# A delta-rule attention with two MoE layers on one core: low words on VectorE, conversions behind the preparation's copies, a MoE lag of two chunks, a fence

## The chip, the cores and the metric

The kernel runs on one core of a Trainium2 chip as a single launch. The metric is device time in microseconds (us). Its engines are PE (TensorE, matmuls; PEld is its weight loads), DVE (VectorE), ACT (ScalarE), POOL (GpSimd) and SP (SyncE, which here only issues transfers). Each engine works through its own list of instructions in order; the lists are bound to each other by semaphores.

## The reference, cut to what matters

```python
# attention, 4 batches x 8 heads, 768 steps, 48 x 48 state per head
y[:, :, t] = q_t @ state
state += beta_t * outer(k_n_t, v_t - state^T k_n_t)
# first layer, 3072 tokens
h = (x @ w1) * (x @ w2) @ w3 @ w_out          # 384 -> 1024 -> 1024 -> 384
# second layer
h = x @ w_in                                   # 384 -> 1024
solu = h * softmax(h)
out = (layernorm(solu) * g_ln) @ w_out2        # 1024 -> 384
```

The weights are 64-bit floats. A piece of them is loaded as two 32-bit words per number, and turned into 32-bit floats on the chip ("conversion").

## The kernel before, in words

Attention is done in chunks of 64 steps (48 chunks, `c`), two at a time: chunks of even and odd `c` belong to two pairs of batches. Three stages share the engines until about 730 us.

**The start (to about 155 us).** `prep(i)` brings k and q of two chunks into the layouts that the chain wants: PE transposes (`pk`, `pq`, lines 258 and 265), ACT copies (260 to 270), products of k with k and q (`pg`, 276), and ACT copies of those (278 to 281, `GD`, `G`). `pk`, `pq` and `pg` share two PSUM buffers. Four such steps fill `GD` for eight chunks, a "set". `invert(n)` then solves 128 triangular systems on DVE in 62 small steps that depend on each other (315, 321), between a transpose of `GD` (`Lz`, 305) and transposes of the result (`Dt` 326, `D1n` 327). Beside all this `conv` steps through the generator `wg`, which converts the weights piece by piece: first `w_out` (8 pieces of 384 columns), then `w3` (16 pieces of 512, transposed on PE as `w3p`, copied as `area`, and multiplied into `w3 @ w_out`, `wps`, line 517, whose result `Ws` is split into two parts by `split`, 217 and 218), then `w1` and `w2` (12 pieces of 512, split in the same way). A piece passes `start` (ACT: the high word, 134; ACT: the low word, 137), `middle` (DVE: a shift, 141) and `finish` (DVE: an add, 178, seen in the profile as CUSTOM_DVE). The pieces share five buffers, so a later load waits until an earlier piece is used up.

**The main loop (chunks two at a time).** `merge` makes the matrices `TW` of a chunk (342 to 381), `chain_u`, `chain_s` and `chain_y` are the recurrence (407, 430, 447, with copies into `X` at 412, 413, 436, 437 and the result `xb` at 457, 458). `load_v`, the copies `kst<-ktok` and the loads of k and q go through SP's queue. The preparation and the inversion of the next set are mixed in. `moe_block(j)` is the first layer for 256 tokens (four chunks): 144 matmuls `pab` (542) and 72 matmuls `px` (562). `fill_moe` hands out its steps. Block `j` may begin in the program when `c_done` has reached `4 * (j + 1) + LAG` and 8 chunks are done.

**The rest** is the end of the first layer and the second layer, where PE has no gaps worth naming.

What sets the order: a tile framework schedules all instructions when the program is built, by their place in the program and a model of their times. An instruction that stands late in the program is put early if its engine is free in that model and its inputs are there. So an edit in one place moves instructions on every engine. `tc.issue_after(ins)` makes all instructions of the block that run on `ins`'s engine stand behind `ins`. `tc.no_sync_barrier()` keeps what stands behind it in the program behind what stands ahead of it, engine by engine, without a semaphore.

Of the kernel before, what the change touches and what calls it, by code (L numbers as in the profile page):

```python
# [8 lines left out]
F32 = mybir.dt.float32  # L9
F32R = mybir.dt.float32r  # L10
U32 = mybir.dt.uint32
I64 = mybir.dt.int64
AF = mybir.ActivationFunctionType
ALU = mybir.AluOpType
# [6 lines left out]
def kernel(  # L21
# [15 lines left out]
    nc = tc.nc  # L37
# [4 lines left out]
    C = 64  # L42
    HC = 32
# [12 lines left out]
    SB = 4  # L56
    CA = 8
    CD = 8
    LAG = 4
    P0, C0 = 4, 24  # L60
    LO = 2
    WO, WB = 2, 15
# [1 line left out]
    KA = 64 + D  # L64
# [32 lines left out]
    QA = at.tile([128, RQ, NP, 2, C], F32, tag="QA", name="QA")  # L97
# [12 lines left out]
    def kt_of(i):  # L110
        return ktoks.get(i, ktok[i % 2])
# [17 lines left out]

    def start(raw, o, n, out):  # L130
        w = raw[:, 2 * o:2 * (o + n)].rearrange("p (n two) -> p n two", two=2)
        low = raw[:, 2 * o:2 * o + n]
        t = out(n)
        nc.scalar.activation(
            out=t, in_=w[:, :, 1].bitcast(F32), func=AF.Prelu, scale=2.0 ** -112, alpha=2.0 ** 32
        )
        nc.scalar.activation(out=low, in_=w[:, :, 0], func=AF.Copy, scale=2.0 ** -29)
        return low, t.bitcast(U32)

    def middle(low, u):  # L140
        nc.vector.tensor_scalar(
# [5 lines left out]
    def convert(items, out, queue=None, behind=0):  # L147

        items = list(items)
        words, holder, pend = {}, {}, []
        nxt = [0]

        def fetch(done, end=len(items)):
            while nxt[0] < end:
                i = nxt[0]  # L160
                slot, parts, w = items[i][:3]
                if slot in holder and holder[slot] >= done:
                    return
                st = slot()[:, 0:2 * w]
                for r, src in parts:
                    d = st.bitcast(I64)[r]
                    if len(src.shape) == 3:
                        d = d.rearrange("p (a d) -> p a d", a=src.shape[1])
                    (queue(i, src) if queue else nc.sync).dma_start(out=d, in_=src)
                words[i] = st.bitcast(U32)  # L170
                holder[slot] = i
                nxt[0] += 1

        def finish():
            i, o, low, u = pend.pop(0)
            n = u.shape[1]
            value = items[i][5](o, n) if len(items[i]) > 5 else low.bitcast(F32)
            nc.vector.tensor_tensor(out=value.bitcast(U32), in0=u, in1=low, op=ALU.add)
            yield
            items[i][4](o, value)  # L180
            yield
            if o + n == items[i][2]:
                fetch(i + 1)

        if behind:
            fetch(0, 1)
            yield
        fetch(0)
        yield
        todo = [(i, o, n) for i, it in enumerate(items) for o, n in it[3]]  # L190
        ahead = []
        for z in range(len(todo) + behind):
            if z < len(todo):
                i, o, n = todo[z]
                if i not in words:
                    while ahead:
                        i2, o2, st = ahead.pop(0)
                        got = yield from middle(*st)
                        pend.append((i2, o2) + got)
                    while pend and i not in words:  # L200
                        yield from finish()
                    fetch(i - 1)
                ahead.append((i, o, start(words[i], o, n, out)))
            if len(ahead) > behind or z >= len(todo) and ahead:
                i, o, st = ahead.pop(0)
                got = yield from middle(*st)
                pend.append((i, o) + got)
                if len(pend) > 1:
                    yield from finish()
        while pend:  # L210
            yield from finish()
# [43 lines left out]
    def prep_t(i):  # L255
        pk = ps_prep.tile([128, NP, 128], F32, tag="prep", name="pk")
        for p in range(NP):
            nc.tensor.transpose(pk[:, p, :], kt_of(i)[:, p, :], ident)
        r = pk.rearrange("r p (c t) -> r c p t", c=2)
        nc.scalar.copy(out=KQ[0:KA, :, :, 0:C], in_=r[0:KA])  # L260
        nc.vector.tensor_copy(out=KB[0:D, :, :, C:128], in_=r[0:D])
        nc.scalar.copy(out=KB[64:KA, :, :, 0:C], in_=r[64:KA])  # L262
        pq = ps_prep.tile([128, NP, 128], F32, tag="prep", name="pq")
        for p in range(NP):
            nc.tensor.transpose(pq[:, p, :], qt_of(i)[:, p, :], ident)
        r = pq.rearrange("r p (c t) -> r c p t", c=2)
        nc.scalar.copy(out=KQ[0:KA, :, :, C:128], in_=r[0:KA])
        sl = chunk_of(i) % RQ
        nc.scalar.copy(out=QA[0:64, sl:sl + 3:2, :, 1, :], in_=r[0:64])
        nc.scalar.copy(out=QA[64:KA, sl:sl + 3:2, :, 0, :], in_=r[64:KA])  # L270

    def prep_g(c):
        cc, sl, u0 = c % 4 // 2, c % RQ, c % SETC * NP
        pg = ps_prep.tile([128, NP, 128], F32, tag="prep", name="pg")
        for p in range(NP):
            nc.tensor.matmul(pg[:, p, :], KB[0:KA, cc, p, :], KQ[0:KA, cc, p, :], start=True, stop=True)  # L276
        gd = GD[:, u0:u0 + NP, :]
        nc.scalar.copy(out=gd[:, :, :], in_=pg[:, :, 0:HC])
        nc.scalar.copy(out=G21[:, sl], in_=pg[:, :, 0:HC])
        nc.scalar.copy(out=gd[32:64], in_=pg[32:64, :, HC:C])  # L280
        nc.scalar.copy(out=gd[96:128], in_=pg[96:128, :, HC:C])  # L281
        for h in range(2):
            r = slice(64 * h, 64 * h + 64)
            nc.vector.tensor_tensor(  # L284
                out=QA[r, sl, :, h, :], in0=pg[r, :, C:128],
                in1=mask[r].unsqueeze(1).to_broadcast([64, NP, C]), op=ALU.mult,
            )
# [362 lines left out]
    for h in range(2):  # L650
        nc.gpsimd.affine_select(
            out=mask[64 * h:64 * h + 64], in_=mask[64 * h:64 * h + 64], pattern=[[1, C]],
# [5 lines left out]
    c_done = [0]  # L658
    acc = [0.0]

    def conv(x, ins=None):
        acc[0] += x
        if acc[0] < 1:
            return
        with (tc.issue_after(ins.ins) if ins is not None and c_done[0] >= CA else nullcontext()):
            while acc[0] >= 1:
                next(wg, None)
                acc[0] -= 1
# [24 lines left out]
    for i in range(SETC // 2):  # L693
        for k_, _ in enumerate(prep(i)):
            if k_ == 0 and i > 0 and i + 1 < SETC // 2:
                norm(i + 1)
            conv(P0)

    for ins in invert(0):
        conv(0.5, ins)  # L700
    invert_end(0)
# [5 lines left out]
    def moe_all():  # L707
        for j in range(NTB):
            while c_done[0] < min(CPT * (j + 1) + LAG, NCH) or c_done[0] < CD:
                yield "wait"  # L710
# [12 lines left out]

    PLAN, PLAN0 = ((0,), (1,), (2, 3), ()), ((), (0, 1), (2, 3), ())
    inv_gen = iter(())
    for c in range(0, NCH, 2):
        n, s = c // SETC, c % SETC
        last = s == SETC - 2
# [214 lines left out]
```

## Time and profile before

| what | us |
|---|---|
| median of 3 runs | 958.99 (954.17 to 960.03) |
| profiled execution, its own time | 959.24 |
| its span, first to last instruction | 957.5 |
| PE busy in the span | 871.8 |
| DVE busy | 597.8 |
| ACT busy | 552.4 |

The mean granted clock of TensorE is 0.959 of full speed. The span is shorter than the time of the execution by 1.74 us. A busy PE is one that has a matmul under way, at whatever clock.

### The profile page before, as it was taken

Reading aid. Unit: us, or ns where it says so; the run is one execution under the profiler, and the core shown is the slowest. Engines: PE = TensorE matmul, PEld = TensorE weight load, DVE = VectorE, ACT = ScalarE, POOL = GpSimd, SP = SyncE. Lnnn points to the kernel's source line nnn. Section 1 sums busy time; section 2 is a strip of 40 time slices with the busy share of each in tenths; the row PEclk is TensorE's granted clock in tenths of the full one; section 3 lists DMA queues with packets and bytes.
Section 4 is the critical chain, followed back from the end, with each engine's and each line's share of the span. In section 5 each row is a group of like instructions: output and inputs, shape, how many; then the busy total and the mean of one; then the engine's idle time right before and its main releaser. Section 6 shows DMA issues by size and latency. Waiting matters only on the chain.

```text
span 957.5 us, 23008 instructions
## 1 busy us (share of the span) xinstructions
PE 871.8 (91%) x9104; PEld 775.8 (81%) x9104; DVE 597.8 (62%) x1500; ACT 552.4 (58%) x1481; POOL 43.7 (5%) x99
## 2 busy tenths in 40 slices
PE   2788669998899899989999999999999999999998
PEld 2554457897789788978888888879999989999997
DVE  5677743695379657944597559765653655555553
ACT  6984688727673786376635873585643444343433
POOL 5100000000000000000000000000000100000000
PEclk9999757999799999997999999999999999999999
DMA  9799313320242133222220321133422212122110
GB/s 242 254 200 151 58 28 58 67 50 11 55 88 45 35 63 66 48 49 54 54 55 22 65 43 36 50 91 96 147 69 84 67 58 66 60 73 67 58 34 34
DMA packets 141691, 70.65 MB, mean 74 GB/s; under 512 B 109712, under 2 KB 133520, under 8 KB 139792
## 3 DMA queue, kind: packets, MB, share of 16 engines
q1 hardware_dynamic: 139808, 57.64, 26.6%
q0 software_dynamic: 1776, 11.54, 3.5%
q8 instruction: 72, 1.18, 0.5%
q14 instruction: 35, 0.29, 0.1%
HBM read 47.91 MB, written 14.25 MB: 65 GB/s over the span
## 4 chain that ended last, share of the span: by engine, by line
PE 33%; issue 22%; ACT 18%; DVE 16%; DMA 7%; POOL 2%; SPq 1%; POOLq 0%; ACTq 0%; DVEq 0%
PE pab L542 10%; PE px L562 6%; ACT TW L342 4%; DVE Tt L321 3%; DVE tmp L315 3%; PE uy L407 3%; PE pm L376 2%; DMA ktok<-in_k_dram 2%; PE wps L517 2%; DVE asg L550 1%; PE pst L430 1%; DMA raw_w2s<-in_moe_w_dram 1%; PE pg L276 1%; PE uy L447 1%; PE ph L833 1%
## 5 line engine op out<-in xcount | busy, mean ns | idle before, releaser
L542 PE MATMUL pab<-xb,w1s 128*128 128x256 f32 x864 | 132.0, 291 | 2.2 <-DVE asg L550 2.1
L542 PE MATMUL pab<-xb,w2s 128*128 128x256 f32 x864 | 129.2, 288 | 0.0
L562 PE MATMUL px<-gh,Ws 128*128 128x256 f32 x864 | 126.7, 293 | 2.1 <-DVE xs L218 1.6
L542 PEld LDWEIGHTS pab<-xb,w1s 128*128 128x128 f32 x864 | 114.3, 193 | 5.3 <-DVE asg L550 3.2
L562 PEld LDWEIGHTS px<-gh,Ws 128*128 128x128 f32 x864 | 110.4, 193 | 7.1 <-DVE xs L218 3.3
L542 PEld LDWEIGHTS pab<-xb,w2s 128*128 128x128 f32 x864 | 113.4, 192 | 1.3
L886 PE MATMUL po<-w4s,ln 128*128 128x384 f32 x576 | 105.7, 339 | 0.3 <-ACT ot L892 0.3
L833 PE MATMUL ph<-wis,x 128*128 128x512 f32 x432 | 105.7, 398 | 0.0
L886 PEld LDWEIGHTS po<-w4s,ln 128*128 128x128 f32 x576 | 101.4, 188 | 2.8 <-ACT ot L892 0.5
L833 PEld LDWEIGHTS ph<-wis,x 128*128 128x128 f32 x432 | 79.5, 189 | 16.9 <-issue 0.2
L849 ACT ACTIVATE e<-ph,nm 128x1024 f32<-128x1024 f32 x24 | 26.8, 1117 | 87.5 <-DVE nm L848 86.0
L342 ACT COPY TW<-Dt 32x128 f32<-32x128 f32 x192 | 56.7, 295 | 15.7 <-DVE Dt L326 12.9
L321 DVE TENSOR_TENSOR Tt<-Tt,tmp 128x31 f32<-128x31 f32 (+15 forms) x186 | 63.1, 340 | 3.5
L315 DVE TENSOR_TENSOR tmp<-Lz,Tt 128x31 f32<-128x31 f32 (+15 forms) x186 | 63.0, 338 | 3.5 <-DVE xp L355 0.2
L549 ACT COPY asg<-pab 128x256 f32<-128x256 f32 x96 | 35.6, 371 | 48.5 <-PE pab L542 42.9
L551 ACT CAST gh<-asg 128x256 fp32r<-128x256 f32 x96 | 38.9, 405 | 37.7 <-DVE asg L550 37.2
L284 DVE TENSOR_TENSOR QA<-pg,mask 64x256 f32<-64x256 f32 x96 | 40.5, 422 | 31.9 <-ACT GD L281 29.3
L276 PE MATMUL pg<-KQ,KB 112*128 112x128 f32 x384 | 53.8, 293 | 3.1 <-ACT KB L262 2.4
L276 PEld LDWEIGHTS pg<-KQ,KB 112*128 112x128 f32 x384 | 49.3, 205 | 7.4 <-ACT KB L262 5.6
L848 DVE TENSOR_REDUCE nm<-ph 128x1 f32<-128x1024 f32 x24 | 29.4, 1225 | 40.4 <-PE ph L833 40.4
L517 PE MATMUL wps<-area 128*128 128x384 f32 x128 | 47.1, 518 | 4.7 <-ACT area L512 2.6
L550 DVE TENSOR_TENSOR asg<-pab,asg 128x256 f32<-128x256 f32 x96 | 40.5, 422 | 17.4 <-ACT asg L549 15.3
(147 smaller groups left out, 1379.6 us busy)
## 6 DMA issues: line engine op xcount, KB each, us to landing
x2d<-xs SPq DMA_DIRECT2D x72, 128.0 KB
x<-x2d SPq DMA_DIRECT2D x24, 384.0 KB
X<-in_v_dram SPq DMA_DIRECT2D x96, 48.0 KB
out_dram<-ot SPq DMA_DIRECT2D x24, 192.0 KB
ktok<-in_k_dram SPq DMA_DIRECT2D x44, 96.0 KB
qtok<-in_q_dram SPq DMA_DIRECT2D x44, 96.0 KB
kst<-ktok SPq DMA_DIRECT2D x88, 48.0 KB
raw_w2s<-in_moe_w_dram POOLq DMA_DIRECT2D x4, 1024.0 KB, 10.3
```

Of the source, the lines that this page charges most:

```text
L276: nc.tensor.matmul(pg[:, p, :], KB[0:KA, cc, p, :], KQ[0:KA, cc, p, :], start=True, stop=True)
L284: nc.vector.tensor_tensor(out=QA[r, sl, :, h, :], in0=pg[r, :, C:128], in1=mask[r].unsqueeze(1).to_broadcast([64, NP, C]), op=ALU.mult,)
L315: yield nc.vector.tensor_tensor(out=t, in0=Lz[:, j, j + 1:HC].unsqueeze(2).to_broadcast([128, m, j + 1]), in1=Tt[:, j, 0:j + 1].unsqueeze( ...
L321: yield nc.vector.tensor_tensor(out=Tt[:, j + 1:HC, 0:j + 1], in0=Tt[:, j + 1:HC, 0:j + 1], in1=t, op=ALU.add)
L342: nc.scalar.copy(out=TW[r, tw, :, g // 2, o:o + HC], in_=Dt[r, us, :])
L517: nc.tensor.matmul(acc[m], w3t[:, j, :], wos[kk // (NF // 2)][:, kk % (NF // 2), :], start=(kk == 0), stop=(kk == NF - 1),)
L542: nc.tensor.matmul(pab[:, e, :], ws[m][:, a, fs], xb[:, b, m, :], start=(n == 0), stop=(n == 3 * NM - 1), skip_group_check=True,)
L550: nc.vector.tensor_tensor(out=g, in0=pab[:, 1, :], in1=asb, op=ALU.mult)
L551: nc.scalar.copy(out=gh[:, 0, f, :], in_=g)
L562: nc.tensor.matmul(px, Ws[:, a, f, js], gh[:, b, f, :], start=(n == 0), stop=(n == 3 * NF - 1),)
L833: nc.tensor.matmul(ph[:, gs], x2[:, m, a, :], wis[:, b, m, gs], start=(n == 0), stop=(n == 3 * NM - 1),)
L886: nc.tensor.matmul(po, ln[:, a, f, :], w4s[:, b, f, :], start=(n == 0), stop=(n == 3 * NF - 1),)
```

## The change: what it does

Four edits.

- In `start` the low word (`w[:, :, 0]`, scaled and rounded to an integer) is made by DVE instead of ACT, into the tile `t`, which before took the high word. The high word is written by ACT over the raw words. `t` and the raw area change their roles in `middle` and `finish`.
- While `held[0]` is set, what `conv` issues on ACT stands behind the last copy that `prep_t` or `prep_g` has issued. `held[0]` is cleared before the first inversion.
- `LAG` goes from 4 to 2.
- A fence stands at the head of the main loop.

```diff
-    LAG = 4
+    LAG = 2
...
     def start(raw, o, n, out):
         w = raw[:, 2 * o:2 * (o + n)].rearrange("p (n two) -> p n two", two=2)
-        low = raw[:, 2 * o:2 * o + n]
-        t = out(n)
+        high = raw[:, 2 * o:2 * o + n]
+        t = out(n).bitcast(U32)
+        nc.vector.tensor_scalar(
+            out=t, in0=w[:, :, 0], scalar1=2.0 ** -29, scalar2=None, op0=ALU.mult
+        )
         nc.scalar.activation(
-            out=t, in_=w[:, :, 1].bitcast(F32), func=AF.Prelu, scale=2.0 ** -112, alpha=2.0 ** 32
+            out=high.bitcast(F32), in_=w[:, :, 1].bitcast(F32), func=AF.Prelu,
+            scale=2.0 ** -112, alpha=2.0 ** 32,
         )
-        nc.scalar.activation(out=low, in_=w[:, :, 0], func=AF.Copy, scale=2.0 ** -29)
-        return low, t.bitcast(U32)
+        return t, high
...
-            value = items[i][5](o, n) if len(items[i]) > 5 else low.bitcast(F32)
+            value = items[i][5](o, n) if len(items[i]) > 5 else u.bitcast(F32)
...
-        nc.scalar.copy(out=QA[64:KA, sl:sl + 3:2, :, 0, :], in_=r[64:KA])
+        held[0] = nc.scalar.copy(out=QA[64:KA, sl:sl + 3:2, :, 0, :], in_=r[64:KA])
...
-        nc.scalar.copy(out=gd[96:128], in_=pg[96:128, :, HC:C])
+        held[0] = nc.scalar.copy(out=gd[96:128], in_=pg[96:128, :, HC:C])
...
-        with (tc.issue_after(ins.ins) if ins is not None and c_done[0] >= CA else nullcontext()):
+        with (tc.issue_after(ins.ins) if ins is not None and c_done[0] >= CA else tc.issue_after(held[0].ins) if held[0] is not None else nullcontext()):
...
+    held[0] = None
     for ins in invert(0):
...
     inv_gen = iter(())
+    tc.no_sync_barrier()
     for c in range(0, NCH, 2):
```

In the changed kernel a line number is higher by 3 from `start` on (278 is 281 there), and by 5 to 7 after `conv`. The new DVE instruction has line 134, the high word on ACT line 137.

ACT, behind the first preparation's copies of q (`QA<-pq`): `stage_a` and `raw_w2s` are weights that are being converted, `GD` and `G_93` the copies of the first `pg`. Before, in the order of the list:

```order
L134 ACTIVATE t<-stage_a 128x384 x2
L137 ACTIVATE stage_a<-stage_a 128x384 x2
L134 ACTIVATE t<-raw_w2s_163 128x384 x2
L137 ACTIVATE raw_w2s_163<-raw_w2s_163 128x384 x2
L134 ACTIVATE t<-raw_w2s_165 128x384 x2
L137 ACTIVATE raw_w2s_165<-raw_w2s_165 128x384 x2
L278 COPY GD<-pg 128x128
L279 COPY G_93<-pg 128x128
L280 COPY GD<-pg 32x128
L281 COPY GD<-pg 32x128
```

And now:

```order
L243 ACTIVATE sq<-early 128x384
L245 ACTIVATE ss<-ss 128x8
L137 ACTIVATE stage_a<-stage_a 128x384
L281 COPY GD<-pg 128x128
L282 COPY G_93<-pg 128x128
L283 COPY GD<-pg 32x128
L284 COPY GD<-pg 32x128
L137 ACTIVATE stage_a<-stage_a 128x384
L137 ACTIVATE raw_w2s_163<-raw_w2s_163 128x384
```

The copies of `pg` stood behind all eight pieces of `w_out`; now they stand behind three.

DVE, from the first `X` copy of the main loop on (`chain_u` of chunk 0). Before, the copy of chunk 1 is three rows further on:

```order
L413 COPY X<-uy 64x4x48
L178 ISA stage_a<-t,stage_a 128x1024
L218 TENSOR_TENSOR w2s_951<-stage_a,w2s_951 128x512
L413 COPY X<-uy 64x4x48
L218 TENSOR_TENSOR w2s_951<-stage_a,w2s_951 128x512
```

Now (the first twelve rows; the copy of chunk 1 is the 29th):

```order
L416 COPY X<-uy 64x4x48
L144 TENSOR_SCALAR raw_w2s_697<-raw_w2s_697 128x512
L221 TENSOR_TENSOR w1s_922<-raw_w2s_647,w1s_922 128x512
L181 ISA raw_w2s_647<-raw_w2s_647,t 128x1024
L134 TENSOR_SCALAR t<-stage_a 128x512
L144 TENSOR_SCALAR raw_w2s_697<-raw_w2s_697 128x512
L181 ISA raw_w2s_697<-raw_w2s_697,t 128x1024
L221 TENSOR_TENSOR w1s_922<-raw_w2s_647,w1s_922 128x512
L134 TENSOR_SCALAR t<-stage_a 128x512
L221 TENSOR_TENSOR w1s_937<-raw_w2s_697,w1s_937 128x512
L144 TENSOR_SCALAR raw_w2s_697<-raw_w2s_697 128x512
L181 ISA raw_w2s_697<-raw_w2s_697,t 128x1024
```

The last pieces of `w1`, which were converted during the first inversion, stand behind the fence, and with those of `w2` between the two `X` copies.

PE, between the steps of `merge` for chunks 28 and 29 (`pm`). Before:

```order
L562 MATMUL px<-gh,Ws 128x256 x5
L360 MATMUL pm<-xp,D1n 32x32 x8
L542 MATMUL pab<-xb,w2s_966 128x256 x2
L542 MATMUL pab<-xb,w2s_989 128x256 x3
L542 MATMUL pab<-xb,w1s_814 128x256 x3
L360 MATMUL pm<-xp,D1n 32x32 x8
L542 MATMUL pab<-xb,w1s_921 128x256 x3
L376 MATMUL pm<-TW,kst 48x64 x8
L542 MATMUL pab<-xb,w1s_936 128x256
L376 MATMUL pm<-TW,kst 48x64 x8
```

And now (a part of it; from the last `pst` of chunk 27 to the first `uy` of chunk 28 there are 101 `pab` in all):

```order
L363 MATMUL pm<-xp,D1n 32x32 x8
L545 MATMUL pab<-xb,w1s_814 128x256 x3
L545 MATMUL pab<-xb,w1s_922 128x256 x3
L545 MATMUL pab<-xb,w1s_937 128x256 x2
L363 MATMUL pm<-xp,D1n 32x32 x8
L545 MATMUL pab<-xb,w1s_937 128x256
L545 MATMUL pab<-xb,w2s_952 128x256 x3
L545 MATMUL pab<-xb,w2s_967 128x256 x3
L545 MATMUL pab<-xb,w2s_990 128x256 x3
```

From the first `uy` of chunk 26 to that of chunk 28 there were 12 `pab` and 14 `px`, now 106 `pab`. It is alike from chunk 34 to 36 and from 42 to 44 (20 and 13 `pab` before, 119 and 112 now). From chunk 10 to 12 there were 9 of the two together, now 23. Between the last `pg` of a set and the first `pm` that needs its inversion the number of MoE matmuls stays within 9 of what it was (249 and 249, 253 and 244, 248 and 246 for three of the sets).

## Rows read from the trace of the kernel before

**Rows 1.** The page: its first line, and busy time by engine.

```profile
span 957.5 us, 23008 instructions
PE 871.8 (91%) x9104; PEld 775.8 (81%) x9104; DVE 597.8 (62%) x1500; ACT 552.4 (58%) x1481; POOL 43.7 (5%) x99
```

**Rows 2.** Windows of the start: length; busy PE, PEld, DVE, ACT, POOL; clock, DMA, GB/s.

```profile
10.75:62.06 51.31, 35.23 (x161) 26.21 (x162) 34.48 (x71) 46.58 (x107) 10.56 (x19) 1.00 0.91 250
62.06:108.14 46.08, 35.01 (x120) 20.68 (x118) 39.59 (x103) 22.52 (x44) 2.46 (x5) 0.92 0.89 150
110.04:154.96 44.92, 33.08 (x528) 28.24 (x529) 16.39 (x31) 38.63 (x110) 0.96 (x1) 0.54 0.17 32
```

**Rows 3.** Timeline: start, duration, engine, line [idle before, releaser].

```profile
24.47 0.27 ACT L278 COPY GD<-pg 128x128 f32<-128x128 f32 x1
26.61 1.09 PE L258 MATMUL pk<-ident,ktok 128*128 128x128 f32 x4 [10.06 <-ACT GD L281]
39.49 1.96 SPq L299 DMA_DIRECT2D bl<-bd  x4
```

**Rows 4.** Chain of waits: start, duration, what.

```profile
66.84 13.86 DMA raw_w2s<-in_moe_w_dram
390.36 1.81 DMA xb<-xb
```

**Rows 5.** Timeline of ACT and DVE around the first inversion and the first chunks.

```profile
60.88 0.26 ACT L281 COPY GD<-pg 32x128 f32<-32x128 f32 x1
62.06 2.00 DVE L305 STREAM_TRANSPOSE Lz<-GD 128x1024 f32<-128x1024 f32 x1
81.50 0.43 DVE L141 TENSOR_SCALAR t<-t 128x512 uint32<-128x512 uint32 x1 [2.95 <-ACT t L134]
108.14 1.90 DVE L326 STREAM_TRANSPOSE Dt<-Tt 128x1024 f32<-128x1024 f32 x1
120.49 0.36 DVE L413 COPY X<-uy 64x192 f32<-64x192 f32 x1
154.08 0.53 ACT L412 COPY X<-uy 64x192 f32<-64x192 f32 x2
```

**Rows 6.** Groups by shape, to 140 us: busy, ns of one | idle.

```profile
L137 ACT ACTIVATE raw_w2s<-raw_w2s 128x512 uint32<-128x512 uint32 x14 | 9.0, 673 | 0.0
L141 DVE TENSOR_SCALAR t<-t 128x512 uint32<-128x512 uint32 x28 | 12.7, 456 | 18.6 <-ACT t L134 17.9
L178 DVE CUSTOM_DVE_ANT_0 raw_w2s<-t,raw_w2s 128x1024 uint16<-128x1024 uint16 x14 | 9.4, 686 | 1.2 <-ACT raw_w2s L137 1.0
L218 DVE TENSOR_TENSOR w1s<-raw_w2s,w1s 128x512 fp32r<-128x512 f32 x6 | 4.1, 687 | 0.0
L217 ACT CAST w1s<-raw_w2s 128x512 fp32r<-128x512 f32 x6 | 3.6, 619 | 3.6 <-PE wps L517 1.8 <-DVE raw_w2s L178 1.7
```

**Rows 7.** Timeline of DVE: the instruction after the first transpose.

```profile
64.28 1.22 DVE L308 SCALAR_TENSOR_TENSOR Lz<-Lz,bl 128x1024 f32<-128x1024 f32 x1
```

**Rows 8.** Windows of chunks 10, 18, 26 and 34.

```profile
233.72:255.16 21.44, 17.96 (x314) 15.14 (x310) 9.53 (x27) 15.51 (x50) 0.00 (x0) 0.81 0.25 47
333.72:347.75 14.03, 12.95 (x241) 11.26 (x241) 7.87 (x21) 12.34 (x40) 0.00 (x0) 1.00 0.28 55
425.78:443.07 17.29, 16.07 (x240) 13.95 (x239) 8.38 (x22) 12.31 (x39) 0.00 (x0) 0.77 0.30 62
533.43:547.90 14.47, 13.94 (x254) 12.57 (x253) 9.31 (x25) 12.32 (x40) 0.00 (x0) 1.00 0.35 72
```

**Rows 9.** Windows of 4 us around the second fall of the clock in the loop.

```profile
432.00:436.00 4.00, 2.78 (x66) 2.43 (x62) 3.06 (x9) 3.77 (x15) 0.00 (x0) 0.87 0.17 29
436.00:440.00 4.00, 4.00 (x45) 3.42 (x44) 2.46 (x8) 2.33 (x10) 0.00 (x0) 0.50 0.24 46
```

**Rows 10.** Waits of PE from 228 to 700 us: total, times, longest.

```profile
PE pm L360 <- DVE xp L355: 9.4, 18, 1.5
```

**Rows 11.** Window of the last chunks, where `w_in` is converted.

```profile
624.00:672.00 48.00, 46.09 (x743) 41.58 (x737) 28.35 (x81) 34.65 (x107) 0.00 (x0) 1.00 0.34 96
```

More of the change, by code (lines that the diff above doesn't have):

```diff
@@ L659 @@
     acc = [0.0]
+    held = [None]
     def conv(x, ins=None):
```

## The prediction

> **What bounds the kernel now.** I read the page first [rows 1]: PE is busy for 871.8 of 957.5 us, so all that a reordering can win is 85.7 us of idle PE, and time in which PE is busy at the lower clock. Next come windows of each stage. About half of the idle time lies ahead of 155 us, the rest almost all in the loop between 190 and 700 us; behind that PE has no gaps. So two questions decide: when the start lets the loop go (its mark is the `X` copy of chunks 4 and 5, at 154.08 [rows 5]), and at which clock and with how few gaps the loop runs.
>
> The start is bound by three lists one after the other [rows 2]. To `Lz` it is ACT: 46.58 of 51.31 us busy. The next `pk` waits 10.06 us for the `GD` copies, which stand in ACT's list behind all of `w_out`'s conversions [rows 3]; the last `GD` copy ends at 61.1 and `Lz` starts at 62.06 [rows 5]. Through the inversion it is DVE: 39.59 of 46.08 us busy in 103 instructions. The largest part of the rest is a stall of 2.95 us in front of the first `w1` piece [rows 5]: its transfer takes 13.86 us and lands at 80.7 [rows 4]. From 110 to 155 it is ACT again, 38.63 of 44.92, while DVE has only 16.39.
>
> [...]
>
> **The change part by part.** All sums stand against the profiled execution, 959.24 us, which is the median of the runs (958.99) to within 0.25.
>
> *Conversions behind the preparation's copies.* The first `GD` copy now stands behind three pieces of `w_out` instead of eight. Five pieces at two passes of some 0.6 us are 6 us: it comes at about 18.6 instead of 24.47, and `pk` follows. But the gain isn't carried whole to `Lz`. The copy `Tt<-bl` (line 310) now stands ahead of the copies of the last two preparations, and `bl` is issued by SP only from 39.49 to 41.45 [rows 3]; with a small transfer's 1.81 us [rows 4] it is there at about 43.5. Behind it are some 30 ACT instructions, about 12.5 us of list. So the last `GD` ends near 56, `Lz` starts near 57: 5 us earlier. The other end: a wait for `bl` that costs all of it, 0.
>
> *The low word on DVE.* ACT loses 36 passes in the start (8 of 384 columns, 28 of 512; 0.673 us each [rows 6]), DVE gains 36 that read every second word. No row shows that operation on DVE. The low bound is a shift of the same 512 columns, contiguous: 0.43 to 0.46 us [rows 5, 6]. The high bound is half of the strided transpose `Lz`, 2.00 us for 1024 [rows 5]: 1.00; the contiguous operation of 1024 right behind it takes 1.22 [rows 7]. I take 0.61, a little less than the two-input subtraction of 512 columns, 0.687 [rows 6], which also reads more than one word per result. Ends kept: 0.43 and 1.00.
>
> [...]
>
> *The inversion.* DVE's list from `Lz` to `Dt` gains nine low words (5.5 us) and one shift (0.46), and loses four subtractions for `w1` (2.75), one for `Ws`, one add (0.69) and the normalisations of two preparations (3.0), which now stand elsewhere: -0.65 us net, so 39 us of busy time and some 2 us of small gaps. In it the first `w1` piece is reached at 74.5 to 76. Its transfer landed at 80.7; it starts when a buffer comes free and SP has issued it, up to 4 us earlier now, so 76 to 80.8; I take 78.4, a stall of about 4 us. `Dt` then starts at 102 to 104 against 108.14: 4.5 us gained of the 5.
>
> *Behind the fence.* The pieces of `w1` and `w2` that now stand between the `X` copies of chunks 0 and 1 on DVE (27 instructions, some 16 us) put the second copy about 25 us behind the start of the loop instead of 10.5 (120.49 less 110.04 [rows 5, 2]). That is covered: ACT's list up to `X(c4,c5)` is longer. It had 38.63 us in 44.92 [rows 2]; six low words leave it (-3.4 to -4), one high word (0.9 with its wait), four casts at 0.62 [rows 6] (2.1 to 2.5), the cast of `Ws` (0.4) and two normalisations (1.4) come to it, so it has 40 to 41.5 us of work, and `X(c4,c5)` comes 42.5 to 43 us behind the loop's start instead of 44. Gain 1.5 us. If DVE's pieces were each 0.4 longer, the cover would be used up. Altogether the start is 6 us shorter; bounds: 9 shorter (no stall for `w1`, cheap low words) and 2 longer (`bl` late, low words near 0.8).
>
> SP's queue: the transfers `kst<-ktok` for chunks 4 and 5 are moved past those of `xb` and the loads of `v`. POOL's: a memset of `Tt` stands in front of one load of weights. Both at nothing: the second set's preparation waits for its normalisation, and the weights for a buffer. If that cover went, each would be one small transfer, 1.8 us [rows 4].
>
> *The low words of `w_in` and `w_out2`* (20 of 256 or 384 columns) lie under a PE that is busy for 46.09 of 48.00 us, with DVE at 28.35 [rows 11]: nothing. Without that cover 20 times 0.3 to 0.6, 6 to 12 us.
>
> *The lag.* The MoE work is the same; only its place moves. Between chunk 26 and 28 there are now 106 `pab` where there were 12 and 14 `px`. At a fall that came when PE had 2.78 us of work in 4 [rows 9] this is the work that was missing. Window 26 lost 17.29 less 14.3, 3 us, and about as much behind it until 450 us: 6.5 us gained. The fall at chunk 10 (21.44 against 14.03) stays, as there are only 23 matmuls of the MoE there now instead of 9, and no block can start before eight chunks are done. PE's waits for `xp` in `merge` are 9.4 us in 18 places [rows 10]; with more MoE work between a few of them I take 1 us. Bounds for the loop: 0 and -14 (both falls gone).
>
> **Sum**: 959.24 - 6 - 6.5 - 1 = 945.7, so 946.
>
> **The rivals.**
>
> 1. *Slower: the low word is dear on DVE.* At 1.00 us instead of 0.61 [rows 5] the 36 of the start cost 14 us more, all of them on the list that bounds the inversion or ahead of the third `X` copy, where the cover is 16 of 42 us. The start is then 8 us longer instead of 6 shorter, and if the loop gives nothing the time is 967. It decides from where -6 + 36 (x - 0.61) = 0, x = 0.78 us. For it: `Lz` against its neighbour [rows 7]. Against: DVE is idle for 16.8 of the 51.31 us ahead of `Lz` [rows 2] and for more behind `Dt`, which take a part. Chance 0.10, 957 to 968.
> 2. *The start gains, the loop doesn't.* The work that is put in at chunk 26 is missing at 28 (36 `pab` there instead of 140), so the fall moves there or to 36 and 44, where now nothing falls [rows 8]. 959.24 - 6 = 953; 950 to 957, chance 0.25.
> 3. *`w1` lands when it did.* The 13.86 us transfer is the same, and if it lands at 80.7 again the inversion keeps all but 2 to 3 us of its old end; the loop gains. 959.24 - 2.5 - 6.5 - 1 = 949.3; 947 to 952, chance 0.15.
> 4. *Both falls go.* 946 less 7 = 939; 935 to 941, chance 0.10. Against: the 23 matmuls.
>
> **How the numbers follow.** My forecast, 946 with 938 to 950 as its own range, has 0.40. The range to hold 8 times in 10 takes in the second and the third rival and the fourth, and the cheap half of the first: 935 to 960. A measurement of this kernel tells 1%, 9.6 us, from no change: faster means under 949.4. That holds nearly all of the forecast, the fourth rival and part of the third: 0.53. Slower, above 968.6, is the dear end of the first rival with a little for what I don't see: 0.07. The rest, 0.40, is no difference that can be told.
>
> **What would show it.** In the changed profile: the first `GD` copy near 18.6 and `Lz` near 57 (the first step); the mean of the new DVE line for 512 columns, 0.61, where 0.78 or more speaks for the first rival; a stall of about 4 us at the first `w1` piece and `Dt` at 102 to 104 (61 or later for `Lz`, 107 or later for `Dt`, and the third rival or worse holds); the second `X` copy far behind the first with nothing waiting, and `X(c4,c5)` near 147 to 148; a granted clock of 1.00 from chunk 26 to 30, with a window of about 14.3 us, and the fall at chunk 10 still there. I am wrong if the clock falls in another pair, if PE is idle between the `X` copies of chunks 0 and 1 because of DVE and the third comes after 154, or if the last set's chunks end later because a MoE block has been used up earlier.

## The result and the profile after

The changed kernel takes 941.30 us (median of 4 executions, 939.07 to 942.89), the one before 956.58 (953.57 to 960.03): a ratio of 0.9845, 95% interval 0.9804 to 0.9886. In the last set of experiments the same kernel took 944.39 against 956.38, with a ratio of 0.9845 (0.9793 to 0.9897). A ratio here is an estimate from the single executions, without those more than 1.5% above the fastest of their kernel, and not the quotient of the two medians, which for this second set would be 0.9875. The forecast was 946.

The page of the profile after, its first line and the busy time by engine, against [rows 1]:

```profile
span 940.7 us, 23008 instructions
PE 864.9 (92%) x9104; PEld 770.7 (82%) x9104; DVE 613.0 (65%) x1556; ACT 525.9 (56%) x1425; POOL 43.6 (5%) x99
```

The span is 16.8 us shorter. PE's busy time fell by 6.9 us and its idle time, span less busy, from 85.7 to 75.8. ACT lost 26.5 us of work and DVE gained 15.2.

The windows that answer to [rows 2, 8] (length; busy PE, PEld, DVE, ACT, POOL; clock, DMA share, GB/s): to `Lz`; from `Lz` to `Dt`; from the first `TW` copy to the `X` copy of chunk 5; on to the second `Lz`; 30 us with the fall of the clock in the loop; and 40 us in which chunk 26 lies.

```profile
12.71:60.85 48.14, 34.82 (x156) 26.77 (x157) 34.04 (x81) 33.69 (x81) 10.26 (x19) 1.00 0.94 253
60.85:101.38 40.53, 33.94 (x123) 20.31 (x122) 37.12 (x100) 14.66 (x26) 2.46 (x5) 1.00 0.98 174
103.34:145.90 42.56, 29.52 (x549) 25.24 (x550) 28.42 (x57) 39.77 (x114) 0.96 (x1) 0.60 0.07 14
145.90:177.03 31.13, 29.55 (x402) 26.64 (x402) 16.88 (x41) 27.95 (x88) 0.00 (x0) 1.00 0.47 90
205.00:235.00 30.00, 28.61 (x400) 25.04 (x399) 16.02 (x41) 17.98 (x58) 0.95 (x1) 0.77 0.08 18
406.00:446.00 40.00, 38.57 (x598) 34.49 (x596) 19.40 (x50) 30.48 (x95) 0.00 (x0) 1.00 0.26 55
```

Up to `Lz` ACT is busy for 33.69 of 48.14 us, where it had 46.58 of 51.31. The inversion is 40.53 us long instead of 46.08. The third row is the stage in which ACT was the bound; it is still busy for 39.77 of 42.56. In the loop this execution has one fall (0.77 between 205 and 235 us, at chunk 8; the two falls before lay at chunks 10 and 26), and chunk 26 runs at 1.00. Its pair is not shorter for that: from its first `uy` (418.39) to that of chunk 28 (441.74) it is 23.35 us, with 106 `pab` in it, where before it was 17.29.

The marks on ACT and on DVE, in the timeline (start, duration, engine, line; in brackets the idle time before and what ended it), against [rows 3, 5]:

```profile
20.26 0.27 ACT L281 COPY GD<-pg 128x128 f32<-128x128 f32 x1
43.22 0.25 ACT L310 COPY Tt<-bl 128x32 f32<-128x32 f32 x1 [0.37 <-issue]
46.40 0.48 ACT L220 CAST Ws<-wps 128x384 fp32r<-128x384 f32 x1 [2.93 <-PE wps L520]
...
142.67 0.30 ACT L415 COPY X<-uy 64x192 f32<-64x192 f32 x1
145.59 0.31 ACT L415 COPY X<-uy 64x192 f32<-64x192 f32 x1
```

```profile
60.85 1.96 DVE L308 STREAM_TRANSPOSE Lz<-GD 128x1024 f32<-128x1024 f32 x1
79.53 0.43 DVE L134 TENSOR_SCALAR t<-raw_w2s 128x512 uint32<-128x512 uint32 x1 [2.24 <-DMA raw_w2s<-in_moe_w_dram]
...
101.38 1.93 DVE L329 STREAM_TRANSPOSE Dt<-Tt 128x1024 f32<-128x1024 f32 x1
112.54 0.36 DVE L416 COPY X<-uy 64x192 f32<-64x192 f32 x1 [4.80 <-ACT X L415]
128.64 0.36 DVE L416 COPY X<-uy 64x192 f32<-64x192 f32 x1
```

The first `GD` copy comes at 20.26 instead of 24.47, `Lz` only 1.2 us earlier than before, `Dt` 6.8 earlier, the `X` copy of chunk 4 11.4 earlier (chunk 5, which before was copied in one row with it, 8.8). The second `X` copy on DVE stands 16.1 us behind the first with conversions between them; ACT is idle for only 2.8 us of the stage, so its list should hide that, but no run moves these pieces alone. The second `Lz` is at 177.03 against 185.38: 8.3 us of the 16.8 are won by then.

The new instruction, by shape up to 140 us (busy, mean ns of one | idle before), with the shift of the same 512 columns and the high word on ACT, against [rows 6]:

```profile
L134 DVE TENSOR_SCALAR t<-raw_w2s 128x512 uint32<-128x512 uint32 x14 | 6.4, 468 | 2.2 <-DMA raw_w2s<-in_moe_w_dram 2.2
L144 DVE TENSOR_SCALAR raw_w2s<-raw_w2s 128x512 uint32<-128x512 uint32 x14 | 5.8, 420 | 3.5 <-ACT raw_w2s L137 3.4
L137 ACT ACTIVATE raw_w2s<-raw_w2s 128x512 f32<-128x512 f32 x14 | 9.2, 671 | 4.5 <-DVE t L134 4.4
```

The low word, which reads every second word, takes some 420 ns, as the contiguous shift does. The mean of 468 comes from one of the 14, which took 1.09 us (at 105.39, while POOL's memset of `Tt`, 0.96 us, ran); the 12 on `stage_a` have a mean of 421.

### The profile page after: what moved, and what is told of

It is laid out like the page before. It is cut to its first block, busy times and chain, and to the rows that moved or that the text cites. A ratio compares the mean times of both kernels' runs of the same rounds, so it can differ in the third digit from the quotient of the medians.

```text
span 940.7 us, 23008 instructions
## 1 busy us (share of the span) xinstructions
PE 864.9 (92%) x9104; PEld 770.7 (82%) x9104; DVE 613.0 (65%) x1556; ACT 525.9 (56%) x1425; POOL 43.6 (5%) x99
## 4 chain that ended last, share of the span: by engine, by line
PE 36%; issue 22%; DVE 17%; ACT 16%; DMA 5%; POOL 2%; SPq 1%; POOLq 0%; ACTq 0%; DVEq 0%
PE pab L545 12%; PE px L565 6%; DVE tmp L318 3%; DVE Tt L324 3%; PE uy L410 3%; PE pg L279 3%; ACT TW L345 3%; PE pm L379 2%; PE pst L433 2%; PE uy L450 2%; DMA raw_w2s<-in_moe_w_dram 1%; PE ph L840 1%; POOL vr L870 1%; DVE Lz L308 1%; DVE Dt L329 1%
## 5 line engine op out<-in xcount | busy, mean ns | idle before, releaser
L840 PEld LDWEIGHTS ph<-wis,x 128*128 128x128 f32 x432 | 79.5, 189 | 16.9 <-issue 0.2
L279 PE MATMUL pg<-KQ,KB 112*128 112x128 f32 x384 | 56.0, 298 | 6.8 <-ACT KB L265 4.8
L552 ACT COPY asg<-pab 128x256 f32<-128x256 f32 x96 | 35.6, 371 | 43.4 <-PE pab L545 40.6
L553 DVE TENSOR_TENSOR asg<-pab,asg 128x256 f32<-128x256 f32 x96 | 40.4, 421 | 25.5 <-ACT asg L552 22.7
L855 DVE TENSOR_REDUCE nm<-ph 128x1 f32<-128x1024 f32 x24 | 29.4, 1225 | 40.4 <-PE ph L840 40.4
L555 DVE TENSOR_TENSOR gh<-asg,gh 128x256 fp32r<-128x256 f32 x96 | 40.4, 421 | 16.3 <-ACT gh L554 15.8
```

Source lines behind the costliest of these rows:

```text
L553: nc.vector.tensor_tensor(out=g, in0=pab[:, 1, :], in1=asb, op=ALU.mult)
L555: nc.vector.tensor_tensor(out=gh[:, 1, f, :], in0=g, in1=gh[:, 0, f, :].bitcast(F32), op=ALU.subtract)
L840: nc.tensor.matmul(ph[:, gs], x2[:, m, a, :], wis[:, b, m, gs], start=(n == 0), stop=(n == 3 * NM - 1),)
```

## The experiments

Medians are over 4 to 12 executions each, the ratio is to the kernel before on the same chip. The marks come from one profiled execution each; its clock is that of this execution, so kernels are compared by their marks and by their medians, not by the spans of the profiles. The first 170 us of `change`, `change_again` and `no_lag` follow the same order of work, and their marks still lie up to 3.3 us (`Dt`) and 2.6 us (second `Lz`) apart: a smaller difference of marks tells nothing.

| kernel | median us | ratio (95%) | `Lz` | `Dt` | `X` of chunk 4 | second `Lz` |
|---|---|---|---|---|---|---|
| before | 956.4 to 957.8 | 1 | 62.1 | 108.1 | 154.1 | 185.4 |
| change | 941.3 | 0.9845 (0.9804, 0.9886) | 60.9 | 101.4 | 142.7 | 177.0 |
| change_again | 944.4 | 0.9845 (0.9793, 0.9897) | 60.6 | 104.7 | 145.2 | 179.6 |
| no_lag | 940.6 | 0.9821 (0.9779, 0.9863) | 60.4 | 103.3 | 144.0 | 178.5 |
| no_held | 950.4 | 0.9931 (0.9897, 0.9966) | 59.6 | 107.2 | 148.8 | 183.2 |
| no_low | 965.5 | 1.0078 (1.0045, 1.0112) | 72.7 | 109.1 | 157.8 | 189.8 |
| no_fence | 963.0 | 1.0069 (1.0041, 1.0097) | 76.7 | 120.5 | 162.4 | 194.1 |
| only_lag | 958.2 | 0.9998 (0.9970, 1.0026) | 61.9 | 108.5 | 154.5 | 186.2 |
| only_low | 965.0 | 1.0062 (1.0032, 1.0093) | 74.6 | 119.3 | 160.3 | 192.2 |
| only_held | 960.5 | 1.0026 (0.9995, 1.0058) | 73.1 | 113.9 | 159.6 | 191.1 |
| only_fence | 959.0 | 1.0005 (0.9973, 1.0037) | 62.9 | 101.1 | 150.4 | 182.3 |
| norm_behind_gd | 954.9 | 0.9975 (0.9943, 1.0007) | 60.7 | 108.6 | 151.8 | 183.7 |
| no_low_bl_late | 957.4 | 0.9997 (0.9960, 1.0034) | 61.8 | 104.1 | 153.6 | 185.7 |
| cast_dve | 946.1 | 0.9870 (0.9831, 0.9908) | 60.4 | 99.5 | 142.1 | 173.6 |

None of the four edits shows a gain alone, and leaving out any one but the lag loses more than half of the gain or all of it.

**The lag.** Left out, and alone:

```diff
# no_lag: the change, but
-    LAG = 2
+    LAG = 4
# only_lag: the kernel before, but
-    LAG = 4
+    LAG = 2
```

> The change with LAG back at 4; the start is that of the change. Theory (start and lag are two separate gains): the second fall of the clock, near chunk 26, comes back and costs 6.5 us, so 948 (946 to 950), with the second Lz still at 177. Rival (the fall at chunk 26 depends on when the loop reaches it, and went because the start became shorter): no fall at 26, 941 to 943.

> The kernel before with LAG 2 and nothing else. Theory (start and lag are two separate gains): chunk 26 keeps a granted clock of 1.00, 950 (948 to 952), start as before. Rival (the fall depends on when the loop reaches chunk 26): the fall is still there or in another pair, 955 to 958.

Measured: 940.6 without it, 958.2 with nothing else. The lag is worth nothing that can be told. The windows of two stretches of `only_lag` and then of `no_lag` show why:

```profile
420.00:440.00 20.00, 18.88 (x376) 16.23 (x371) 9.50 (x25) 16.77 (x55) 0.00 (x0) 1.00 0.29 63
510.00:530.00 20.00, 18.65 (x242) 16.30 (x242) 10.03 (x25) 10.71 (x37) 0.96 (x1) 0.70 0.10 28
```

```profile
420.00:440.00 20.00, 19.11 (x244) 17.50 (x245) 12.28 (x33) 15.26 (x48) 0.00 (x0) 0.91 0.32 65
510.00:530.00 20.00, 19.07 (x331) 16.68 (x330) 10.91 (x30) 15.93 (x52) 0.00 (x0) 1.00 0.32 65
```

With the lag at 2 in the kernel before, the fall at 430 us is gone (1.00), but there is one at 510 to 530 (0.70) where none was in that execution of the kernel before. With the lag at 4 in the change, 420 to 440 has 0.91, a short fall, and the time is the same. Two executions of the changed kernel itself, the first profile and `change_again`, differ as much:

```profile
205.00:235.00 30.00, 28.61 (x400) 25.04 (x399) 16.02 (x41) 17.98 (x58) 0.95 (x1) 0.77 0.08 18
595.00:625.00 30.00, 27.20 (x444) 23.56 (x443) 21.40 (x58) 20.24 (x67) 0.00 (x0) 1.00 0.28 78
```

```profile
205.00:235.00 30.00, 27.06 (x430) 23.87 (x428) 18.81 (x50) 19.85 (x63) 0.95 (x1) 1.00 0.10 21
595.00:625.00 30.00, 28.56 (x408) 25.04 (x407) 18.66 (x51) 17.98 (x59) 0.00 (x0) 0.77 0.25 70
```

So a fall that one execution shows need not be in the next. My theory of two separate gains failed on both sides. The rival put up against it (the fall depends on when the loop reaches chunk 26) fits `no_lag` in time, at 940.6 a little under the 941 to 943 that it gave, though a short fall at chunk 26 was there, and it fits `only_lag` at 958.2, a little over its 955 to 958.

**The fence.** Left out, alone, and replaced by an order for the normalisations only:

```diff
# no_fence: the change, but
-    tc.no_sync_barrier()
     for c in range(0, NCH, 2):
# norm_behind_gd: as no_fence, and
+    gdl = held[0]                      # the last GD copy of the first set
     held[0] = None
...
-                norm(i)                # in extra()
+                with tc.issue_after(gdl.ins) if n == 0 else nullcontext():
+                    norm(i)
# only_fence: the kernel before, but
+    tc.no_sync_barrier()
     for c in range(0, NCH, 2):
```

> The change without the fence. Seven pieces go back into the inversion on DVE. Theory (the pieces cost DVE about 8 us there and take as much away behind Dt, where ACT's list covers them): Dt near 109, second X copy on DVE a few us behind the first, X of chunks 4 and 5 within 3 us of 142.7, second Lz within 3 us of 177, 941 to 945. Rival (the fence is where the start's gain comes from): X of chunks 4 and 5 at 150 or later, 948 to 952.

> The kernel before with the fence and nothing else. Theory (pieces taken out of the inversion come back behind the first X copy on an ACT that is full there): Dt 4 to 6 us earlier, X of chunks 4 and 5 within 2 us of 154, 955 to 959. Rival (a shorter inversion is a shorter start): X of chunks 4 and 5 at 149 or earlier, 950 to 953.

> The change without the fence, but the main loop's first two normalisations stand on ACT behind the last GD copy of the first set. Theory (the fence is worth so much because without it a normalisation stands in ACT's list ahead of GD and waits 13.3 us for ktok): Lz back at 60 to 62 from 76.7, Dt at 105 to 109, since the pieces of w1 stay in the inversion, X of chunks 4 and 5 at 146 to 151, 943 to 950. Rival (what counts is that the fence takes pieces of w1 out of the inversion): 955 to 963.

`no_fence` was 963.0, slower than either value. The timeline of its ACT and DVE:

```profile
57.27 0.52 ACT L243 ACTIVATE sq<-ktok 128x384 f32<-128x384 f32 x1 [13.29 <-DMA ktok<-in_k_dram]
```

```profile
76.73 1.96 DVE L308 STREAM_TRANSPOSE Lz<-GD 128x1024 f32<-128x1024 f32 x1
```

`sq<-ktok` is the first instruction of a normalisation of the main loop. Without the fence it stands ahead of the last `GD` copies in ACT's list and waits 13.29 us for a load of k. Everything that ACT holds behind it is late, and `Lz` starts at 76.73 instead of 60.85. `norm_behind_gd` takes that wait away: `Lz` is back at 60.7, 16 us earlier. The time falls only from 963.0 to 954.9 (on two chips; 9 us by the ratios). One part of what is missing is that its inversion, 47.94 us, is longer than that of `no_fence` (43.73, from `Lz` to `Dt`). Some 12 us by the ratios are left to the change, and its windows of the inversion and of the stage behind it show where part of them are:

```profile
60.68:108.62 47.94, 36.46 (x125) 21.21 (x123) 44.72 (x121) 19.64 (x37) 2.46 (x5) 0.94 0.90 155
110.60:151.80 41.20, 32.22 (x524) 27.40 (x525) 17.75 (x34) 34.99 (x102) 1.37 (x1) 0.50 0.17 32
```

The pieces of `w1` stay in the inversion: 121 DVE instructions instead of 100, 44.72 us busy instead of 37.12, and `Dt` comes at 108.6. Behind it the stage is hardly shorter (41.2 us) although ACT has only 34.99 us to do; the clock there is 0.50 throughout (0.60 in the change), and what bounds the stage is not shown. So the fence has two effects of about 9 and 12 us. `Lz` and `Dt` came where my theory put them, but I had nearly all of the time on the first effect (943 to 950); the measured time is the rival's (955 to 963), which had it on the second. Alone, with the low words still on ACT, the fence shortens the inversion about as much (38.21 us, 46.08 before), and then:

```profile
62.88:101.09 38.21, 31.21 (x113) 18.83 (x112) 32.36 (x84) 16.33 (x31) 2.45 (x5) 0.96 0.99 166
103.10:150.40 47.30, 30.18 (x525) 25.26 (x524) 24.84 (x48) 42.28 (x115) 0.96 (x1) 0.58 0.12 22
```

The stage behind it is 47.30 us long with ACT busy for 42.28 (before: 44.0 us): 3 us are left at the second `Lz`, and no time: 959.0, as the theory had it, though its marks (154 for `X`, 4 to 6 us for `Dt`, which came 7 earlier) were not met.

**The low words.** Left out, alone, and left out with the copy of `bl` moved:

```diff
# no_low: the change with start() and finish() of the kernel before
# only_low: the kernel before with start() and finish() of the change
# no_low_bl_late: as no_low, and in invert(0)
-        nc.scalar.copy(out=Tt..., in_=bl[:, n, :])
+        with tc.issue_after(gdl[0].ins) if n == 0 else nullcontext():   # gdl[0]: the last GD copy
+            nc.scalar.copy(out=Tt..., in_=bl[:, n, :])
```

> The change with the low words back on ACT. Theory (ACT's list bounds the start, so its 36 passes of 0.6 us matter): 17 of them stand ahead of the last GD copy, Lz comes 3 to 6 us later than in the change (64 to 67), X of chunks 4 and 5 at 150 or later, 947 to 950. Rival (ACT has room enough once the copies come first): Lz within 1 us of 60.9, 941 to 943.

> The kernel before with the low words on DVE and nothing else. Theory (ACT's list bounds the start up to Lz; the order alone matters little): ACT loses 21 passes ahead of the last GD copy, Lz within 1 us of the change's 60.9, Dt near 109 because DVE has all pieces in the inversion, second Lz 5 to 8 us earlier than before (177 to 180), 949 to 952. Rival (the low words only move work to DVE, which bounds the inversion): Dt later than 108 by 3 us or more, 956 to 960.

> The change with the low words on ACT, as in no_low, but the copy of bl into Tt stands on ACT behind the last GD copy. Theory (in no_low that copy waits 9.2 us for bl ahead of the last preparations): Lz at 63 to 66 instead of 72.7, the rest as slow as in no_low (46.7 us from the first TW copy to X of chunk 5), 955 to 959. Rival (Lz is late there by ACT's own work): Lz at 70 or later, 962 to 966.

`no_low` was 965.5, worse than I had expected. ACT and DVE in its timeline:

```profile
44.43 0.25 ACT L307 COPY Tt<-bl 128x32 f32<-128x32 f32 x1 [9.21 <-DMA bl<-bd]
```

```profile
72.69 2.00 DVE L305 STREAM_TRANSPOSE Lz<-GD 128x1024 f32<-128x1024 f32 x1
```

Here the `Tt` copy stands ahead of the `GD` copies of the last four chunks and waits 9.21 us for `bl`. With it moved behind the last `GD` copy, ACT and DVE run

```profile
61.50 0.23 ACT L308 COPY Tt<-bl 128x32 f32<-128x32 f32 x1
```

```profile
61.83 2.00 DVE L305 STREAM_TRANSPOSE Lz<-GD 128x1024 f32<-128x1024 f32 x1
```

without that wait: `Lz` at 61.8, 10.9 us earlier, and 957.4, as expected (955 to 959). The rest of what the low words cost on ACT shows behind the inversion: 47.5 us from the first `TW` copy to the `X` copies of chunks 4 and 5 (one row), against 42.2 to that of chunk 5 in the change. Alone, the low words on DVE gave 965.0. ACT has less to do, and a normalisation now stands ahead of the last `GD` copies, where it waits (that the model which sets the order found ACT free there is my reading; no run shows the model):

```profile
55.43 0.52 ACT L243 ACTIVATE sq<-ktok 128x384 f32<-128x384 f32 x1 [8.24 <-DMA ktok<-in_k_dram]
```

It is the same wait as in `no_fence`. I had not expected it (949 to 952); the rival's 956 to 960, with the inversion as the bound, was also too low.

**The order behind the preparation's copies.** Left out, and alone:

```diff
# no_held: the change, but in conv()
-        with (... else tc.issue_after(held[0].ins) if held[0] is not None else nullcontext()):
+        with (... else nullcontext()):
# only_held: the kernel before with held[0] as in the change, and its line in conv()
```

> The change without the order of conversions behind the preparation's copies. Theory (in the change Lz waits for the last two preparations and for wps, not for the first GD copy): the first GD copy comes 3 us later, Lz at most 1 us later, 941 to 943. Rival (each us of the first GD copy is a us of Lz): Lz at 64, 944 to 945.

> The kernel before with the conversions behind the preparation's copies and nothing else. Theory (ACT has as many passes ahead of the last GD copy, 34 instead of 41): Lz 2 to 4 us earlier, Dt the same or later, since four pieces more fall into the inversion: 954 to 957. Rival (the order is the start's gain): Lz 5 us earlier and Dt too, 950 to 952.

`no_held` was 950.4, slower than both values, although its `Lz` is the earliest of all. Its DVE:

```profile
59.57 1.99 DVE L308 STREAM_TRANSPOSE Lz<-GD 128x1024 f32<-128x1024 f32 x1
70.76 0.36 DVE L318 TENSOR_TENSOR tmp<-Lz,Tt 128x192 f32<-128x192 f32 x1
80.90 0.43 DVE L134 TENSOR_SCALAR t<-raw_w2s 128x512 uint32<-128x512 uint32 x1 [9.78 <-DMA raw_w2s<-in_moe_w_dram]
...
107.18 1.97 DVE L329 STREAM_TRANSPOSE Dt<-Tt 128x1024 f32<-128x1024 f32 x1
```

More pieces are converted ahead of `Lz`, so fewer stand between `Lz` and the first `w1` piece, and DVE reaches that piece after 15 of the 62 steps instead of 19. The transfer lands at 80.9, about as late as in the change (79.5 and 80.5 in two executions), and DVE stands still for 9.78 us in front of it instead of 2.24 to 3.51, with the steps of the inversion behind it. What is won ahead of `Lz` is lost there, and more. Alone, the order gave 960.5 (954 to 957 expected): it puts the copy of `bl` too early, and a normalisation too:

```profile
44.43 0.25 ACT L307 COPY Tt<-bl 128x32 f32<-128x32 f32 x1 [9.09 <-DMA bl<-bd]
57.01 0.52 ACT L240 ACTIVATE sq<-ktok 128x384 f32<-128x384 f32 x1 [2.80 <-DMA ktok<-in_k_dram]
```

**The casts.** An addition to the change:

```diff
-    def split(src, hi, lo):
-        nc.scalar.copy(out=hi, in_=src)
+    def split(src, hi, lo, cast=None):       # cast: nc.vector.tensor_copy for w2
+        (cast or nc.scalar.copy)(out=hi, in_=src)
```

> The change with the six casts of w2 (split, high part) on DVE instead of ACT. Theory (from the first TW copy to X of chunk 5 ACT has no gap: 42.2 us of work in 42.2): six casts of 0.62 us leave it, X of chunk 5 comes 2 to 4 us earlier after TW, the second Lz 1 to 3, 938 to 941. Rival (the stage is bound by the chain of X copies, or DVE between the first two X copies becomes the bound): no earlier, 941 to 944.

> The change itself, on the chip of these three. If the lag is worth nothing, as the comparison of no_lag (940.6) with the change (941.3) says, its many executions lie about 941 with 40 to 50 us at the lower clock, as those of no_lag did (32 to 66). If the lag is worth 2 us or more, the median is 938 or less; if it costs as much, 944 or more.

The window of its stage from the first `TW` copy to the `X` copies:

```profile
101.50:142.10 40.60, 25.67 (x523) 22.20 (x524) 29.87 (x62) 36.13 (x107) 0.96 (x1) 0.66 0.08 16
```

The stage is 40.6 us long instead of 41.5 to 42.2, with `X` of chunk 5 at 142 against 146 to 148, and the second `Lz` 3.5 to 6 us earlier. But at most 1.6 us of that are the stage's, where the theory had 2 to 4: ACT is busy there for 36.13 us, some 3 less than in the change, so its list is not the whole bound. The rest lies ahead of the stage: `Dt` starts at 99.5, because in this execution the first `w1` piece landed at 77.7 (79.5 to 80.5 in those of the change). The median is 946.1 beside 944.4 for the change on that chip; their ranges overlap, and no gain is seen at the end. It is no better version. `change_again` lies at the upper of the two bounds that I had set: if the lag does anything, it costs, but its executions spent 66 us at the lower clock where I had expected 40 to 50, and the ratios of the two kernels (0.9845 and 0.9821) have intervals that overlap over most of their length, so this isn't shown.

## Why the prediction was right, and where it was wrong

**The start: right, with parts that were off.** I took 6 us. At the second `Lz` it is 8.3 in the first profile, 6.9 in `no_lag` and 5.8 in `change_again`, which have the same start; at the `X` copy of chunk 5 it is 8.8, 7.4 and 6.2.

- The first `GD` copy came at 20.26 (18.6 predicted), and `Tt<-bl` at 43.22 (43.5). But `Lz` came at 60.85 instead of 57: from `Tt<-bl` to the last `GD` copy ACT is busy for 11.1 us, a little less than the 12.5 that I reckoned, but the list takes 16.1, as it also waits, first and longest 2.93 us for `wps` (46.40 in the timeline). I costed that list without its waits.
- The low word: 0.42 us instead of 0.61, so at the low bound of what I kept. The read of every second 32-bit integer costs here no more than the contiguous shift, 421 to 420 ns for 512 columns, and half of the strided transpose `Lz`, 1.00 us, which I had kept as the high end, was far off.
- The inversion: 40.53 us, predicted 45 to 47. DVE has 37.12 us of work in it where I had 39, which the cheaper low word accounts for, and the stall in front of `w1` is 2.24 instead of 4. (The terms of my list add to about -1.05 with 0.56 for the subtraction for `Ws`, and not to -0.65.) The rest is the execution: in `change_again`, with the clock at 0.92 there, the inversion is 44.10 with the same work on DVE, by a longer stall (3.51) and a wait of 2.21 for `Ws`:

```profile
60.58:104.68 44.10, 36.67 (x123) 21.67 (x122) 37.22 (x100) 14.66 (x26) 2.44 (x5) 0.92 0.89 162
92.68 0.56 DVE L221 TENSOR_TENSOR Ws<-wps,Ws 128x384 fp32r<-128x384 f32 x1 [2.21 <-ACT Ws L220]
```

  The profile before had 0.92 there too. At that clock the gain in the inversion is 46.08 less 44.10, 2 us; the 5.5 us of the first profile hold an execution without a fall as well.
- The transfer of `w1` landed at 79.5 to 80.5; I had taken 78.4. The third rival (it lands where it did, 80.7) was nearly right on the transfer and wrong on its consequence, as later conversions of `w3` fill the time ahead of it.
- The stage behind it: 42.2 us to the `X` copy of chunk 5, predicted 42.5 to 43. (The terms that I listed add to 39.4 to 40.4 us of ACT's work, not 40 to 41.5; measured 39.77.) That DVE's pieces between the two `X` copies cost nothing is argued from ACT's 2.8 us of idle time, as said.

**What I did not see in the edits.** I costed the fence by the pieces that it moves. Its other effect, that it keeps two normalisations out of ACT's list ahead of the last `GD` copies, did not appear in a comparison of before and after, since in neither do they stand there. Only the kernels with some of the edits show it: with the low words off ACT and no fence, an instruction that waits 8.2 to 13.3 us for a transfer stands ahead of the copies. In the same way the order behind the copies lets the `Tt` copy run into its 9.1 to 9.2 us wait when the low words are on ACT. The three edits of the start are one change in three parts.

**The lag: wrong.** The step that failed is "Window 26 lost 17.29 less 14.3, 3 us, and about as much behind it until 450 us: 6.5 us gained." From one execution I took the fall at chunk 26 for a property of the program, and the missing MoE work at that place for its cause. Two executions of the change, with falls at 220 in one and at 330 and 610 us in the other, show that the falls change their place without any edit. `no_lag` has the old MoE order and loses nothing; `only_lag` has the new one and gains nothing, and shows a fall at another pair, as the second rival said in kind (its pairs were 28, 36 and 44; it came at 32). By the sign that I had set for it (the clock falls in another pair) I am wrong there: in the first profile it fell at chunk 8. The length of 14.3 us that I gave to the pair at a granted clock of 1.00 (between the 14.03 and 14.47 of [rows 8]) left out the `pab` that move into it: it measured 23.35. The rest of the 6.5 us, behind the window, was my estimate: in the profile before the clock was 0.50 from 440 to 448 us and 0.92 from 448 to 452. No run shows the 6.5 us as a gain of the lag; `no_lag` and `only_lag` show none. PE's waits for `xp` in `merge` did shrink with the lag, to 7.0 and 6.0 us from 9.1 in `no_lag`, more than the 1 us that I took, but no time went with it.

**What took its place.** Over the executions of these kernels and of the one before, compared within each kernel, one that spends 1 us more at the lower clock (its time, times 1 less its granted clock, times 2, with the 0.50 of [rows 9] taken as the lower clock) is 0.19 us longer. The kernel before spends 81 us there on average, the change 57 (42 in the first four executions, 66 in the last six). By this fit, at an equal 75 us the kernel before would be at about 956.4 and the change at 946.2: 10 us are the schedule's, and 24 us less of low clock go with the other 4.6. `no_lag` would be at 945.1 in the same way. This is an estimate: the fit shows that the two go together, not that the clock is the cause, and the marks place only 5.8 to 8.3 of the 10 us. So that the sum was near is in part luck: the 6 us of the start were earned, and the 7.5 us of the loop, which the lag did not give, were made up by schedule time that I had not placed and by a gain that went with the clock and came without the lag. Why the clock falls less often in the change is open. In the profiled pair 17 us of the 29 less at the lower clock lie ahead of 160 us, but no experiment set the clock apart from the start.

**The first rival** (slower by a dear low word) fell with the 0.42 us. A kernel with a part of the change missing can be slower than the one before, but by another way than I had named: the waits on k and on `bl`.

## What to carry to other kernels

Where instructions are placed by a model of time, taking work off an engine may let in, as it did here (waits of 8.24 us in `only_low` and 13.29 in `no_fence`), an instruction that waits for a transfer ahead of the work that matters; so look, in every version, for the first long wait in the list ahead of the critical copy, and fence it out. In `no_held` DVE came to the first `w1` piece after 15 of the 62 steps instead of 19 and stood still for 9.78 us in front of it: when freeing an engine, see that work which does not depend on the next arrival stands between. A fall of the clock in one profile is no term of a sum until a second execution shows it at the same place.

## What the runs showed of the hardware that was not expected

The low word on DVE, which reads 32-bit integers at every second word and multiplies, takes 421 ns for 512 columns, as long as a shift of contiguous words (420); the next instruction started 0.34 us behind its start (79.53 to 79.87). The strided transpose `Lz` of the profile before, 2.00 us for 1024, was no guide to it. The one low word that ran beside POOL's memset of `Tt` (0.96 us) took 1.09 us (at 105.39), and one behind the inversion 1.08 in `change_again` (108.66) and 1.07 in `cast_dve` (103.55); no run moves the memset, so that it is the cause is not shown.

Executions of one and the same kernel spread over 14 us (949 to 963 for the kernel before on one chip), and their mean granted clock with them: 0.950 to 0.969, which reckoned as above is 59 to 96 us at the lower clock. Between 110 and 150 us, the first chunks, the mean granted clock was 0.54 before, 0.62 in the change and in `change_again`, 0.64 in `no_lag`, 0.50 in `norm_behind_gd`, 0.63 in `no_low_bl_late` and 0.70 in `cast_dve`; before it was 0.50 from 108 to 124 and from 128 to 152 us, in the change from 108 to 140. The falls behind 200 us changed their place from kernel to kernel (248 to 260 and 436 to 448 us before, between 510 and 530 in `only_lag`), and between two executions of the change (between 205 and 235 us in one, between 595 and 625 in the other).
